# Linear attention and a swish feed-forward layer in one kernel: sums of phi(k) by row tiles, and the k-v products two groups earlier

## The chip, the cores and the metric

The kernel runs on one core of a Trainium2 chip. The metric is the device time of one execution in microseconds (us). Seven runs of the kernel before the change gave a median of 289.71 us (288.77 to 290.61). The profile shown here is of one more execution, which took 289.96 us; the span from its first to its last recorded instruction is 288.2 us. All times of the trace are counted from the start of that span.

## The reference

Eight batches, eight heads, 576 tokens and a head width of 64 go through linear attention, and its result through a feed-forward layer (4608 tokens, width 512, inner width 2048):

```python
q_p, k_p = (phi(q), phi(k))               # phi(x) = elu(x) + 1
kv = np.einsum('bhsd,bhse->bhde', k_p, v)
z = np.sum(k_p, axis=2)
num = np.einsum('bhsd,bhde->bhse', q_p, kv)
den = np.einsum('bhsd,bhd->bhs', q_p, z)[..., None] + 1e-06
x = num / den                             # heads side by side: 4608 x 512
h = x @ w_in
g = h * (1.0 / (1.0 + np.exp(-beta * h)))
out = g @ w_out
```

## The kernel before, in words

**Layout.** A batch's 576 tokens are cut into G = 64 groups of J = 9 tokens. Two heads stand on the 128 partitions (64 groups each), and two pairs of heads ("pr" 0 and 1) make up the four head pairs together with the index h. `phi_k` of a batch is a tile of 128 partitions by (pr, j, 128 columns): rows 0 to 63 belong to one head (hh = 0), rows 64 to 127 to another (hh = 1), and the 128 columns hold two more halves (h = 0, 1) of 64 channels each.

**Products of k.** `k_quads` (L177) walks over j, h and hh and multiplies a 64x64 quadrant of `phi_k`, as the weights, with a moving operand of 64 rows. One call is 36 matmuls, each with a weight load of its own. It serves three purposes: `z_products` (L189, batches 0 and 1 only) uses a single column of ones and so sums phi(k) over the tokens; `kv_direct` (L205, batches 0 and 1) multiplies with v; `kv_both` (L224, batches 2 to 7) multiplies with v that has a column of ones beside it, so that one product gives both kv and z.

**Order.** The order of the instructions is written out by hand (manual_schedule), engine by engine in the order of the code. There are three parts:

- The opening (L547 to L689), batch 0: phi of q and k, transposes of phi(q) (`q_trans`), `z_products` (L578 and L583) and `kv_direct` (L580, L645) with dummy matmuls (`idle`) between them, then the numerators by token tiles (`numer_mm`, L593), their division on DVE (`numer_norm`), the transposes of x (`x_part`, L618) and the first four groups of h = x w_in in pieces (`h0_part`, L628).
- Batch 0's second matrix product (`y_mm`, L447) interleaved with the attention of batch 1 (L708 to L756): `q_trans(1, ...)` at L715 and L718, both `z_products(1, pr)` at L723, `kv_direct(1, pr)`, the denominators (`dens`), the numerators (`numer0`, divided on DVE at L392), the transposes of x (`x_trans1`, copied by ACT at L413), and the four output copies `y_out` (L460, DVE copies L239). `y_sb` has three buffers, so the fourth output copy waits for the first one's DMAs.
- The loop over b = 1 to 8 (L799), in which each H phase (`h_phase`, 16 groups of four 512-column matmuls and a Silu on ACT) and each Y phase (`y_phase`) carries pieces of the attention of batch b + 1 and b + 2. `at(sh, n, ...)` hangs a piece behind group n of H, `at(sy, n, ...)` behind step n of Y. `kv_both(n)` hangs behind group index 10 (the eleventh group), `numers(n)` and the divisions `norms(n, k)` behind the last; `x_trans_dma` sends x through transposing DMAs on SP's queue. For b = 2 the left-over tokens of batches 0 and 1 (`odd_numers`, `odd_norms`) hang ahead of kv_both at index 10, and their four transposing DMAs at index 11.

Instructions are fetched while the kernel runs: the page lists a queue q8 of the kind "instruction" with 20 packets and 0.33 MB. PE's program has 2548 weight loads and 2548 matmuls, by far the longest of the engines.

PSUM has four buffers of one bank that H and Y share (`mmps`), and two small pools for the attention. In the loop the odd numerators (`nps_m`) take two of the four shared buffers until `norms(n, 2)` has read them on DVE; the third token tile of Y waits for that. `norms(n, 2)` needs a fourth and fifth `xs` buffer, and the fifth is free when the first transposing DMA of x (`xT<-xs`) has landed.

**Loads.** POOL issues the loads of q, k, v and the weights that convert to bf16 (queue q0); SP issues the transposing DMAs, the outputs and the loads of v from batch 3 on (queue q1). `load_kq(m + 1)` is held until batch m's transposes of phi(q) (`qTd`, L269) have landed.

Of the kernel before, what the change touches and what calls it, by code (L numbers as in the profile page):

```python
# [16 lines left out]
def kernel(  # L17
# [10 lines left out]
    nc = tc.nc  # L28
# [7 lines left out]
    G = 64  # L36
    J = S // G
# [72 lines left out]
    ones = consts.tile([P, 2], BF16)  # L110
# [27 lines left out]
    st = {}  # L138
# [23 lines left out]
    def places(b, pr):  # L162

        return slice(2 * pr, 2 * pr + 2) if b < 2 else slice(pr, 4, 2)
# [6 lines left out]
    def v_copy(eng, b, pr):  # L171
        src = vb[b % 2] if b == 2 else vf[b % 2]
        eng.tensor_copy(  # L173
            vaug[b % 2][:, pr, :, :, 0:D], src[:, places(b, pr)].rearrange("p h j d -> p j h d")
        )

    def k_quads(b, pr, dst, mov):  # L177

        for j in range(J):
            for h in range(2):  # L180
                for hh in range(2):
                    r = slice(hh * G, (hh + 1) * G)
                    c = slice(h * D, (h + 1) * D)
                    nc.tensor.matmul(  # L184
                        dst[hh][c], st[b, "k"][r, pr, j, c], mov(r, j, h),
                        start=(j == 0), stop=(j == J - 1), skip_group_check=True,
                    )

    def z_products(b, pr, ps):  # L189

        k_quads(b, pr, [a[:, 256 + pr : 257 + pr] for a in ps], lambda r, j, h: ones[r, 0:1])

    def z_evac(b, ps):
        for hh in range(2):
# [26 lines left out]
    def num_tile(name):  # L221
        return numps.tile([P, 2, 512], F32, tag="num", name=name)

    def kv_both(b):  # L224

        t = num_tile("kvp")
        for pr in range(2):
            k_quads(
                b, pr, [t[:, hh, pr * EA : (pr + 1) * EA] for hh in range(2)],
                lambda r, j, h: vaug[b % 2][r, pr, j, h, 0:EA],  # L230
            )
        st[b, "kvd"] = work.tile([P, 2, 2 * EA], BF16, tag="kv_bd", name="kvd")
        nc.vector.tensor_copy(st[b, "kvd"], t[:, :, 0 : 2 * EA])  # L233
# [32 lines left out]
    def q_trans_dma(b):  # L266
        st[b, "qTd"] = work.tile([P, 4 * J, G], BF16, tag="qT", name="qTd")
        for hh in range(2):
            st[b, "qTd", "dma"] = nc.sync.dma_start_transpose(  # L269
                out=st[b, "qTd"][:, hh * 2 * J : (hh + 1) * 2 * J],  # L270
                in_=st[b, "q"][hh * G : (hh + 1) * G].rearrange("p a j c -> p (a j c)"),
            )

    def q_odd_trans(b, tp):

        tv = tp.rearrange("p (a n) -> p a n", a=2)
        for pr in range(2):
            nc.tensor.matmul(
                tv[:, pr], st[b, "q"][:, pr, J - 1, :], identity,
                is_transpose=True, start=True, stop=True, skip_group_check=True,  # L280
            )
        nc.scalar.copy(
            q_odd[b].rearrange("p (i a) g -> p a i g", i=2),
            tv.rearrange("p a (i g) -> p a i g", i=2),
        )
# [30 lines left out]
    def numers(b):  # L316
        pairs = [num_tile("nps") for _ in range(2)]
        odd = [mm_tile("nps_m") for _ in range(2)]
        for k in range(2):
            dst = [pairs[k][:, h] for h in range(2)]  # L320
            numer_tile(b, dst, k)
            numer_tile(b, dst, 2, (k,), 4)
        numer_tile(b, odd, 3)
        for hh in range(2):
            quads(b, odd, 4 + hh, lambda c: (c, J - 1), hh, None)
        st[b, "nps"] = pairs, odd
# [36 lines left out]
    def norms(b, k):  # L363

        den = work.tile([P, 2, 6], F32, tag="den", name="den")
        rden = work.tile([P, 2, 6], F32, tag="rden", name="rden")
        pairs, odd = st[b, "nps"]
        if k < 2:
            nv = pairs[k][:, :, 0 : 6 * EA].rearrange("p h (n e) -> p h n e", e=EA)
            nc.vector.tensor_scalar(den, nv[:, :, :, D], 1e-6, None, ALU.add)  # L370
            nc.vector.reciprocal(rden, den)
            x = xs_tile(b, k).rearrange("p (h n) d -> p h n d", h=2)
            scale(x, nv[:, :, 0:4, 0:D], rden[:, :, 0:4])
            if k == 0:
                xs_tile(b, 2)
            x = st[b, "xs", 2].rearrange("p (h n) d -> p h n d", h=2)
            scale(x[:, :, 2 * k : 2 * k + 2], nv[:, :, 4:6, 0:D], rden[:, :, 4:6])
            return
        nv = [a[:, 0 : 6 * EA].rearrange("p (n e) -> p n e", e=EA) for a in odd]
        for h in range(2):  # L380
            nc.vector.tensor_scalar(den[:, h], nv[h][:, :, D], 1e-6, None, ALU.add)
        nc.vector.reciprocal(rden, den)
        x = xs_tile(b, 3)
        for h in range(2):
            scale(x[:, 4 * h : 4 * h + 4], nv[h][:, 0:4, 0:D], rden[:, h, 0:4])
        x = xs_tile(b, 4)
        for h in range(2):
            scale(x[:, 2 * h : 2 * h + 2], nv[h][:, 4:6, 0:D], rden[:, h, 4:6])
# [9 lines left out]
    def x_dst(b, t):  # L398
        if t < NT - 1:
            return xT[b % 3][:, :, t * P : (t + 1) * P]  # L400
        return xT_tail[:, :, b * G : (b + 1) * G]
# [15 lines left out]
    def x_trans_dma(b, t):  # L417
        xv = st[b, "xs", t].rearrange("p n d -> p (n d)")
        if t < NT - 1:
            nc.sync.dma_start_transpose(out=x_dst(b, t), in_=xv)  # L420
            return

        for pr in range(2):
            nc.sync.dma_start_transpose(
                out=xT_tail[:, places(b, pr), b * G : (b + 1) * G],
                in_=xv[pr * G : (pr + 1) * G, 0 : 2 * P],
            )
# [39 lines left out]
    def load_kq(b, after=None):  # L467
        if b < B:
            d = load(nc.gpsimd, xq[b % NX], q, b)
            if after is not None:  # L470
                hold(d, after)
            load(nc.gpsimd, xk[b % NX], k, b)

    def load_v(b):
        if b < B:
            load(nc.sync, vf[b % 2], v, b)

    def phi_all(b, a):
        phi_tile(b, a)
        for pr in range(2):  # L480
            phi_part(b, a, pr, xin(b, a, pr))
        for pr in range(2):
            phi_relu(b, a, pr, xin(b, a, pr))
        for pr in range(2):
            phi_min(b, a, pr)
# [90 lines left out]
    idle(3)  # L576
    zt = [num0_tile() for _ in range(2)]
    z_products(0, 0, zt)  # L578
    idle(2)
    kv_direct(0, 0, kvp0)  # L580
    for hh in range(2):
        kv_evac(0, hh, (0,), kvp0)
    z_products(0, 1, zt)  # L583
    bps = miscps.tile([P, FC], F32, tag="misc", name="bps")
    nc.tensor.matmul(bps, beta_row, ident16, is_transpose=True, start=True, stop=True)
# [137 lines left out]
    for pr in range(2):  # L723
        z_products(1, pr, zt1)
# [46 lines left out]
    def h_phase(b, x, side):  # L771
        for ff in range(FC):
            hp = mm_tile("h_ps")
            h_mm(b, x, ff, hp)
            silu(b, ff, hp)
            run(side, ff)
# [18 lines left out]
    def at(side, n, *fs):  # L795
        side.setdefault(n, []).extend(fs)


    for b in range(1, B + 1):  # L799
        n = b + 1  # L800
        sh, sy = {}, {}
        if b == 1:
            at(sh, 0, lambda: q_trans_dma(2))
            at(sh, 1, lambda: [v_copy(nc.gpsimd, 2, pr) for pr in range(2)])
            at(sh, 2, lambda: q_odd_trans(1, num_tile("qop")[:, 0].bitcast(BF16)[:, 0:256]))
            at(sh, 2, lambda: load_kq(3, st[2, "qTd", "dma"]), lambda: load_v(3))
        if b == 2:
            at(sh, 10, odd_numers, odd_norms)
            at(sh, 11, lambda: [x_trans_dma(i, 4) for i in range(2)])
        if n < B:  # L810
            at(sh, 10, lambda: kv_both(n))
            at(sh, FC - 1, lambda: numers(n), lambda: [norms(n, k) for k in range(3)])
            for t in range(NT):
                at(sy, t // 3, lambda t=t: x_trans_dma(n, t))
        if n + 1 < B:
            m = n + 1
            at(sy, 3, lambda: phi_all(m, "q"))
            at(sy, 5, lambda: q_trans_dma(m), lambda: load_kq(m + 1, st[m, "qTd", "dma"]))
            at(sy, 8, lambda: phi_all(m, "k"), lambda: [v_copy(nc.gpsimd, m, pr) for pr in range(2)])
            at(sy, 9, lambda: load_v(m + 1))  # L820
        h_phase(b, xT[b % 3] if b < B else xT_tail, sh)
        y_phase(b, sy, last=(b == B))
# [30 lines left out]
```

## Time and profile before

| what | us |
|---|---|
| median of 7 runs | 289.71 |
| the profiled execution | 289.96 |
| its span | 288.2 |
| PE busy | 278.7 (97%) |
| ACT busy | 161.3 (56%) |
| DVE busy | 106.2 (37%) |
| POOL busy | 36.8 (13%) |
| PE on the chain that ended last | 88% |
| matmuls of H (L432), share of that chain | 41% |
| matmuls of Y (L450), share of that chain | 40% |

A busy PE is one on which some matmul is recorded; matmuls are pipelined, so a duration of 0.17 us for one matmul does not mean that the next starts 0.17 us later. The time per matmul in a run of equal ones is read from where the run starts and ends: the run's length, less one matmul's duration, divided by their number less one. "issue" as the reason of an idle stretch means that the engine waited for nothing that the profile records. The granted TensorE clock is 1.0 throughout.

### The profile page before, as it was taken

To read this page: it belongs to the slowest core of one execution; us is meant where nothing else is said; L and a number is where in the kernel's file an instruction comes from. 1 tells how busy PE (TensorE), PEld (TensorE's weight loads), DVE (VectorE), ACT (ScalarE), POOL (GpSimd) and SP (SyncE) were. 2 spreads that over 40 slices of the span, in tenths; PEclk is the share of its full clock that TensorE was granted. 3 is DMA by queue.
4 is the path that set the end of the run, shared out by engine and by line. 5 is a ranking of instruction groups with operands and counts; after the bars stand their busy time and mean duration, and the time that the engine had idled before them with its cause. 6 is when DMAs were issued, how large, how long until landed. Compare 5 with 4: busy or idle time off the path is not lost.

```text
span 288.2 us, 6079 instructions
## 1 busy us (share of the span) xinstructions
PE 278.7 (97%) x2548; PEld 136.3 (47%) x2548; DVE 106.2 (37%) x255; ACT 161.3 (56%) x220; POOL 36.8 (13%) x51
## 2 busy tenths in 40 slices
PE   7879998999999999999999999999999999999994
PEld 3574457444444444444445444544454444444443
DVE  5833577535531491039203930293026100110012
ACT  5758775975736852776287717770860086017500
POOL 8632000220013001300140007000000000000000
PEclk9999999999999999999999999999999999999999
DMA  7999999679389728953796379638403410230032
GB/s 219 208 217 392 247 252 170 148 206 218 73 185 282 128 64 176 295 93 79 166 288 107 82 163 282 116 77 131 104 2 81 114 36 0 48 81 19 0 75 74
DMA packets 51725, 41.05 MB, mean 142 GB/s; under 512 B 31585, under 2 KB 43121, under 8 KB 51697
## 3 DMA queue, kind: packets, MB, share of 16 engines
q1 hardware_dynamic: 38800, 23.61, 34.4%
q0 software_dynamic: 12736, 16.91, 29.8%
q8 instruction: 20, 0.33, 0.5%
q10 hardware_dynamic: 160, 0.13, 0.2%
q14 instruction: 9, 0.07, 0.1%
HBM read 36.71 MB, written 9.44 MB: 160 GB/s over the span
## 4 chain that ended last, share of the span: by engine, by line
PE 88%; DMA 6%; DVE 2%; ACT 1%; issue 1%; SPq 0%; DVEq 0%; POOLq 0%
PE h_ps L432 41%; PE y_ps L450 40%; DMA xk<-in_k_dram 2%; DMA xT<-xs 2%; PE kvp L184 2%; DMA out_dram<-y_sb 1%; PE h_ps L632 1%; PE nps L303 1%; DVE xs L392 1%; DVE y_sb L239 1%; PE nps L184 1%; PE warm_ps L133 0%; ACT g L440 0%; PE nps_m L303 0%; ACT e L144 0%
## 5 line engine op out<-in xcount | busy, mean ns | idle before, releaser
L440 ACT ACTIVATE g<-h_ps,beta_c 128x512 bf16<-128x512 f32 x144 | 97.9, 689 | 92.8 <-PE h_ps L432 92.4
L450 PE MATMUL y_ps<-w_out,g 128*128 128x512 bf16 (+3 forms) x600 | 127.4, 371 | 1.3 <-issue 0.9
L432 PE MATMUL h_ps<-xT,w_in 128*128 128x512 bf16 x496 | 109.8, 379 | 0.6 <-ACT xT L413 0.2
L450 PEld LDWEIGHTS <-g 128*128 128x128 bf16 x600 | 57.6, 98 | 65.7 <-issue 1.0
L432 PEld LDWEIGHTS <-w_in 128*128 128x128 bf16 x560 | 54.2, 98 | 65.1 <-issue 1.3
L239 DVE COPY y_sb<-y_ps 128x512 f32<-128x512 f32 (+2 forms) x37 | 24.8, 674 | 76.0 <-PE y_ps L450 72.9
L83 POOL DMA_DIRECT2D xq<-in_q_dram x7 | 5.2, 744 | 109.5 <-ACT g L440 97.0
L144 ACT ACTIVATE e<-xk 128x1152 bf16<-128x1152 bf16 x16 | 17.8, 1152 | 1.7 <-DMA xk<-in_k_dram 1.5
L233 DVE CAST kvd<-kvp 128x260 bf16<-128x260 f32 x6 | 2.6, 426 | 41.5 <-PE kvp L184 41.5
L144 ACT ACTIVATE e<-xq 128x1152 bf16<-128x1152 bf16 x14 | 15.5, 1155 | 0.1
L432 PE MATMUL h_ps<-xT_tail,w_in 128*128 128x512 bf16 x64 | 14.0, 379 | 0.0
L155 DVE TENSOR_TENSOR phi_q<-e,r 128x1152 bf16<-128x1152 bf16 (+2 forms) x17 | 11.7, 717 | 2.7 <-ACT e L144 2.4
L361 DVE TENSOR_TENSOR xs<-nps,rden 128x512 bf16<-128x512 f32 (+1 forms) x24 | 12.2, 552 | 0.4
L155 DVE TENSOR_TENSOR phi_k<-e,r 128x1152 bf16<-128x1152 bf16 x16 | 11.6, 751 | 0.6 <-ACT e L144 0.4
L173 POOL CAST vaug<-vf 128x1152 bf16<-128x1152 f32 x10 | 11.2, 1160 | 2.0 <-DMA vf<-in_v_dram 2.0
L370 DVE TENSOR_SCALAR den<-nps 128x12 f32<-128x12 f32 x12 | 2.0, 164 | 25.4 <-PE nps L303 25.4
L144 ACT ACT_TABLE_LOAD x6 | 7.7, 1283 | 3.4 <-DMA xq<-in_q_dram 3.4
L133 PE MATMUL warm_ps<-xT 128*128 128x512 bf16 x23 | 8.2, 504 | 1.5 <-DVE xT L96 1.5
L184 PEld LDWEIGHTS <-phi_k 64*64 64x64 bf16 x720 | 6.9, 107 | 4.4 <-issue 3.0
L361 DVE TENSOR_TENSOR xs<-nps_m,rden 128x256 bf16<-128x256 f32 (+1 forms) x24 | 7.0, 349 | 4.2 <-DMA xT<-xs 3.4
L440 ACT ACT_TABLE_LOAD x6 | 7.7, 1283 | 0.1
L83 POOL DMA_DIRECT2D xk<-in_k_dram x9 | 6.8, 751 | 4.5 <-DMA g<-in_moe_w_out_dram 1.9
(93 smaller groups left out, 118.0 us busy)
## 6 DMA issues: line engine op xcount, KB each, us to landing
out_dram<-y_sb SPq DMA_DIRECT2D x70, 128.0 KB, 2.4
vf<-in_v_dram SPq DMA_DIRECT2D x5, 1152.0 KB, 6.6
xq<-in_q_dram POOLq DMA_DIRECT2D x7, 576.0 KB, 9.7
xk<-in_k_dram POOLq DMA_DIRECT2D x7, 576.0 KB, 12.3
w_in<-in_moe_w_in_dram POOLq DMA_DIRECT2D x4, 512.0 KB, 12.8
g<-in_moe_w_out_dram POOLq DMA_DIRECT2D x2, 1024.0 KB, 17.3
stage<-in_moe_w_out_dram POOLq DMA_DIRECT2D x2, 1024.0 KB, 19.7
stage<-in_q_dram SPq DMA_DIRECT2D x2, 576.0 KB, 4.1
```

The lines of the kernel that those rows point to most:

```text
L83: return eng.dma_start(out=dst[:, h0 : h0 + n].rearrange("p h j d -> p h (j d)"), in_=rows.rearrange("(i p) e -> p i e", p=P)[:, h0 : h0 + n],
L133: nc.tensor.matmul(warm_ps[:, 0:cols], warm[:, 0:P], warm[:, 0:cols], start=True, stop=True)
L144: nc.scalar.activation(st[b, a, pr, "e"][:, :, j0:j1], x[:, :, j0:j1], ACTF.Exp)
L155: nc.vector.tensor_tensor(st[b, a][:, pr, j0:j1].rearrange("p j (h d) -> p j h d", h=2), st[b, a, pr, "e"][:, :, j0:j1].rearrange("p h j d ...
L173: eng.tensor_copy(vaug[b % 2][:, pr, :, :, 0:D], src[:, places(b, pr)].rearrange("p h j d -> p j h d"))
L184: nc.tensor.matmul(dst[hh][c], st[b, "k"][r, pr, j, c], mov(r, j, h), start=(j == 0), stop=(j == J - 1), skip_group_check=True,)
L239: eng.tensor_copy(dst, src)
L303: nc.tensor.matmul(dst[h][c * G : (c + 1) * G, e * EA : (e + 1) * EA], st[b, "qTd"][r, (hh * 2 + p) * J + j, :], st[b, "kvd"][r, hh, p * E ...
L361: nc.vector.tensor_mul(out, num, rd[..., None].to_broadcast(list(num.shape)))
L432: nc.tensor.matmul(hp[:, c0:c1], w_in_sb[ff // 4][:, kc, (ff % 4) * P : (ff % 4 + 1) * P], x[:, kc, c0:c1], start=(kc == 0), stop=(kc == K ...
L440: nc.scalar.activation(g_sb[b % 2][:, ff, :], hp, ACTF.Silu, scale=beta_c[:, ff : ff + 1])
L450: nc.tensor.matmul(yp[:, c0:c1], g_sb[b % 2][:, ff, t * P : (t + 1) * P], w_out_sb[i][:, c, c0:c1], start=(ff == 0), stop=(ff == FC - 1), ...
```

## The change

`z_products` no longer goes through `k_quads`. It takes 64 rows and all 128 columns of `phi_k` as weights (a row tile), so that both halves h are summed by one matmul: 18 weight loads and 18 matmuls per call where there were 36 of each. There are four calls (batches 0 and 1, two pr each), so PE's program loses 72 weight loads and 72 matmuls. Sums, PSUM places and the instructions that read them (`z_evac`) are the same.

In the loop, `kv_both(n)` moves from behind group index 10 of H to behind index 8, that is from the eleventh to the ninth group, for all b from 1 to 6. For b = 2 `odd_numers` and `odd_norms` move along with it, and the four transposing DMAs of the left-over tokens move from index 11 to 9. `numers(n)` and everything in Y stay.

```diff
     def z_products(b, pr, ps):
 
-        k_quads(b, pr, [a[:, 256 + pr : 257 + pr] for a in ps], lambda r, j, h: ones[r, 0:1])
+        for j in range(J):
+            for hh in range(2):
+                r = slice(hh * G, (hh + 1) * G)
+                nc.tensor.matmul(
+                    ps[hh][:, 256 + pr : 257 + pr], st[b, "k"][r, pr, j, :], ones[r, 0:1],
+                    start=(j == 0), stop=(j == J - 1), skip_group_check=True,
+                )
...
         if b == 2:
-            at(sh, 10, odd_numers, odd_norms)
-            at(sh, 11, lambda: [x_trans_dma(i, 4) for i in range(2)])
+            at(sh, 8, odd_numers, odd_norms)
+            at(sh, 9, lambda: [x_trans_dma(i, 4) for i in range(2)])
         if n < B:
-            at(sh, 10, lambda: kv_both(n))
+            at(sh, 8, lambda: kv_both(n))
```

## The prediction

> **What bounds the kernel now.** I read the page first (PE busy 97%, 88% of the chain), then the chain of waits in order of time. From 75.33 us to the end the chain is PE without a break, one H and Y phase after another, and the change takes no PE work out of that stretch. So what it is worth is decided before 75.33 us. There the chain has these pieces (start, length, what):
>
> ```profile
> 15.33 0.17 PE nps L598 x3
> 15.50 1.37 issue
> 16.86 0.23 PE nps L598
> ...
> 48.69 0.61 DVE y_sb L239
> ...
> 49.91 3.90 DMA out_dram<-y_sb
> ...
> 53.92 0.69 DVE y_sb L239
> ...
> 55.04 0.70 ACT g L440
> ...
> 68.70 6.26 DMA xT<-xs
> 74.96 0.02 issue
> 74.98 0.30 DVE xs L361
> 75.28 0.05 issue
> 75.33 0.82 PE y_ps L450 x3
> ```
>
> Two DMA waits and one idle stretch of PE with no cause on record stand out. The timeline of PE has that stretch and a second one; the other two rows price small matmuls:
>
> ```profile
> 9.86 0.45 PE L184 MATMUL nps<-ones,phi_k 64*64 64x1 bf16 x36 [0.71 <-DVE phi_k L155]
> 12.30 0.54 PE L513 MATMUL dps<-z,qT 128*128 128x2 bf16 x16
> 16.86 0.23 PE L598 MATMUL nps<-kv,qT 128*128 128x128 bf16 x1 [1.37 <-issue]
> 49.51 0.60 PE L450 MATMUL y_ps<-w_out,g 128*128 128x256 bf16 x4 [0.89 <-issue]
> ```
>
> Counted in PE's program (each weight load and each matmul a row), 446 rows precede the first stall and 1,213 the second: 767 apart. The page explains the number:
>
> ```profile
> q8 instruction: 20, 0.33, 0.5%
> ```
>
> 20 packets carry the 5,096 rows, about 256 each; 767 is three times 256 less one wait instruction of PE's sequencer in between. So I read both stalls as PE at the edge of a block of instructions that has not arrived. PE began the blocks before these (rows 190 and 957) at 10.98 and 43.73 and could go on at 16.86 and 49.51: a block arrives 5.8 to 5.9 us after PE has begun the one before it, while loads fill the DMA engines. PE normally takes far longer for 256 rows (108 ns per row in Y, 27 us), but the small matmuls use up rows quickly.
>
> The second stall has a sequel. The DMA view of 50 to 53 us:
>
> ```profile
> q1 hardware_dynamic: 154, 0.25, 36.8%
> q8 instruction: 1, 0.02, 3.6%
> ...
> out_dram<-y_sb SPq DMA_DIRECT2D x3, 128.0 KB, 3.9
> ```
>
> 3.6% of 16 engines over 3 us is 1.7 us: one engine is held by one instruction packet, and the output DMAs of that moment need 3.9 us where the page's median is 2.4. The fourth output copy waits for them (53.92), so does phi of batch 2 on DVE behind it, then `qTd`, then the held loads of batch 3, then the first `xT` (74.96), then Y's third tile (75.33), which PE would have reached 0.45 us earlier.
>
> **The change, part by part.** Block edges stay at the same row numbers; 36 rows of work after each `z_products` come earlier.
>
> *Edge at row 446.* Row 190, which asks for it, is now in the second `z_products`, at 11.3 (it waits for phi_k as before), so the block is there at 17.2. Row 446 is now in `x_part(1, 1)`, which ran at 18.83, without the stall 17.46. The stall of 1.37 us goes. What is late next: w_in lands in time (20.02 for the third quarter, wanted at 23.4), but `q_trans(1)` needs phi_q of batch 1, whose last DVE piece ends at 38.00 because the load of xq landed at 33.63. PE came to it at 38.72. So of 1.37 only 0.66 us reaches batch 1; 0.71 us is slack, which also covers a dearer `z_products` in batch 0.
>
> *Row tiles.* 36 quadrant matmuls take (0.45 - 0.167)/35 = 8 ns each, since four quadrants work side by side: 0.29 us a call. No row of the trace has a 64x128 weight tile. Below: two side by side at half the quadrants' rate is 16 ns, half of the full-array row (dps: (0.54 - 0.163)/15 = 25 ns) 12.5 ns. Above: a whole weight load unhidden, 98 ns (the LDWEIGHTS 128x128 rows). I take 25 ns, the nearest row, whose weights also have 128 columns: 0.45 us a call, +0.16 us. Batch 0's two calls (+0.32) vanish in the slack; batch 1's two cost +0.32. There `kv_direct` follows at once, now with another tile shape: by the chain 72 quadrant matmuls cost 0.71 to 0.73 us where they follow full tiles (kvp) and 0.67 where they follow quadrants (kv), so +0.06. The quadrants' 8 ns per pair shows that weight loads are mostly hidden here. The Trainium skill ("TensorE: Matmul & The Clock Gate", "LDWEIGHTS (loading the stationary operand)") speaks against the change: a load's time goes with its columns, whatever its rows, so half as many loads of twice the columns save nothing; its 107 ns, two side by side, would make a call 0.96 us (an estimate), and the gain of the whole change about 0.1 us.
>
> *Edge at row 957.* Before, row 702 came in plain Y work long ahead. Now it follows `q_trans(1)` at about 38.5, so the block arrives by 44.4 at the latest; PE reaches row 957, near the end of `kv_direct(1)`, at about 44.1. A stall of 0 to 0.3 us; I take 0.15.
>
> *Edge at row 1213.* It moves from the opening into `kv_both(2)`, at some 59 us; the block is there long before. The stall before 49.51 goes: `x_trans1(3)` ran at 50.60 and would have run at 49.56, so 1.04 us. The Trainium skill ("Runtime: NRT & Kernel Launch", "Instruction fetch mechanics") has the blocks of 256 but calls crossing an edge mostly hidden; by that the fewer rows would be worth nothing. The two stalls above say otherwise here.
>
> Sum at `x_trans1(3)`: -0.66 + 0.32 + 0.06 + 0.15 - 1.04 = **-1.17 us**. ACT behind it (copy, exp of k, table load, first Silu, which ended at 55.73 and set H's fifth group at 55.77) shifts alike. PE then reaches Y's third tile at 74.88 - 1.17 = 73.71.
>
> *The DMA side must keep up.* With no block asked for at 49.5, the output DMAs issued at 49.91 - 0.13 should land after 2.4 us, at 52.18 in place of 53.80: the fourth copy starts at 52.3 (-1.62), phi of batch 2, `qTd`, the loads of batch 3 and the landing of `xT` follow by the same: 74.96 - 1.62 = 73.34, and 0.35 us of DVE later the third tile is free at 73.69. So PE's 73.71 sets it, just: 75.33 - 73.71 = **1.62 us gained**.
>
> *kv two groups earlier.* No PE work changes; 16 rows and 1.73 us come between kvp and numers, so that 256 rows across both take at least 7 us, over the 5.9 a block needs. What kvp waits for: vaug of batch 3 ends on POOL at 88.85, kvp would start at 91.99 - 1.73 = 90.26; the later batches have 2 us to spare. In b = 1, phi_k(2) ends at 59.54 - 1.62 = 57.9 and kvp comes at about 59.0; even at the old phi it would wait under 0.6 us, which the third tile's idle time covers. A waiting kvp would hold up H's next group on PE, and Silu on ACT behind it. The four transposing DMAs of b = 2 keep SP busy for 5.58 us from 91.4 in place of 93.10; behind them stand batch 3's at 98.78, which gain 1.7 us of room. DVE has 9 us idle there. I cost this part at nothing; without that room a wait on vaug would cost at most the 1.73 us, once.
>
> **In time.** The profiled execution took 289.96, so 288.3; it lies 0.25 above the median, 289.71. Against that: **288.1 us**.
>
> **Rivals.**
> - *More.* The packet at 32.95 on q8 moves to about 39 us, so xq of batch 1 may land up to 0.95 us sooner, and row tiles may run at 12.5 ns. Then up to 0.6 us less wait and 0.45 us cheaper tiles: as far as the DMA side follows, 287.0 to 287.6. 0.10.
> - *Absorbed.* The output DMAs at 50 us stay at 3.9 us for another reason (loads of v still running until 50.31), and the chain through `xT` moves by 0.1 to 0.3 us only: 289.5. For it: the last load packets and the outputs are close. Against: 2.4 us everywhere else. 0.20.
> - *Slower: weight loads of row tiles not hidden.* With p us each (p over 0.036, where the slack is used up), `x_trans1(3)` shifts by 72p - 3.50 us: four calls of 18, less 144 quadrants at 8 ns (1.15), less 1.37 and 1.04, plus 0.06. The third tile's idle time covers 0.45 of it. It loses from 55 ns each, by over 0.3% from 67 ns, and at 98 ns by 3.1 us: 292.9. Against it: 25 ns with full tiles. 0.08.
>
> The forecast case itself (287.7 to 288.7) has 0.62. 0.3% is 0.87 us, about what a measurement of this kernel can tell from no change: faster by more than that 0.71 (forecast, more), within it 0.20, slower 0.09. The range takes in the first two rivals and tiles of up to 55 ns, and leaves out the slow end: 286.9 to 289.7.
>
> **What would show it.** Right: no idle "issue" near PE rows 446 and 1213; q8 packets no longer between 50 and 53 us; output DMAs there at 2.4 us; the fourth y_sb copy near 52.3; Y's third tile of b = 1 near 73.7 (the 1.62 us); from there on the same spacing of phases (29.3 us) as before. Wrong: 18 row tiles over 0.6 us; a stall of the old size at the new edges; `xT` still landing near 75; kvp waiting for POOL or DVE in any batch.

## The result, and the profile after

| | before | after |
|---|---|---|
| median, us | 289.58 (47 runs, 288.77 to 291.42) | 287.36 (20 runs, 287.06 to 287.91) |
| ratio of the times | 1 | 0.9918, 95% interval 0.9905 to 0.993 |
| the profiled execution, us | 289.96 | 287.37 |
| its span, us | 288.2 | 285.6 |
| weight loads, and as many matmuls | 2548 | 2476 |

The change is worth 2.22 us by the medians and 2.59 us between the two profiled executions (the one of before lay 0.38 above its median). The granted clock has a part in the medians. Of the 82 runs of the kernel before that stand beside the experiments, 29 had a mean granted clock of 0.994 or less and a median of 290.68 us, the other 53 one of 289.30; of the 20 runs of the changed kernel one was at 0.994. At the full clock the change is thus worth some 1.9 us (an estimate, 289.30 less 287.36). One run of the experiments below, at a clock of 0.754 (363.84 us, with quadrants in batch 1), is left out there. The forecast was 288.1 us, 0.74 too high, with 286.9 to 289.7 around it.

The page of the changed kernel has one packet fewer on the instruction queue:

```profile
q8 instruction: 19, 0.31, 0.4%
```

PE's timeline of the opening, where before had 1.37 us of idle "issue" (start, busy time, instruction, and in brackets the idle time ahead of it with its releaser):

```profile
9.57 0.38 PE L194 MATMUL nps<-ones,phi_k 64*128 64x1 bf16 x18 [0.33 <-DVE phi_k L155]
...
10.96 0.38 PE L194 MATMUL nps<-ones,phi_k 64*128 64x1 bf16 x18
...
14.42 0.62 PE L638 MATMUL h_ps<-xT,w_in 128*128 128x128 bf16 x8 [0.25 <-DMA w_in<-in_moe_w_in_dram]
14.87 0.39 PE L604 MATMUL nps<-kv,qT 128*128 128x128 bf16 x4
```

The four matmuls of `numer_mm` (L604) run through with no idle time ahead of them; row 446 now comes at 17.00, in `x_part(1, 1)`. The two `z_products` show the row tile: 18 in 0.38 us, so (0.38 - 0.160)/17 = 12.9 ns each (one such matmul lasts 0.160 us), and the run of 36 below gives (0.60 - 0.160)/35 = 12.6.

The same view around the second stall:

```profile
42.56 0.60 PE L194 MATMUL nps<-ones,phi_k 64*128 64x1 bf16 x36
43.09 0.78 PE L184 MATMUL kv<-vf,phi_k 64*64 64x64 bf16 x72
...
48.41 0.60 PE L456 MATMUL y_ps<-w_out,g 128*128 128x256 bf16 x4
48.85 0.39 PE L414 MATMUL tp<-identity,xs 128*128 128x128 bf16 x4
```

Nothing idle: `x_trans1(3)` starts at 48.85, where it was at 50.60. The DMA view of 50 to 53 us has no row for q8 any more, and the output DMAs are back at the median of the page:

```profile
q1 hardware_dynamic: 364, 0.61, 88.2%
...
out_dram<-y_sb SPq DMA_DIRECT2D x5, 128.0 KB, 2.4
```

DVE's timeline has the fourth output copy 2.2 us sooner (before: 53.92), and it waits 1.90 us for the first one's DMA:

```profile
51.69 0.69 DVE L245 COPY y_sb<-y_ps 128x512 f32<-128x512 f32 x1 [1.90 <-DMA out_dram<-y_sb]
```

The chain of waits, in order of time (start, length, what):

```profile
33.86 1.28 ACT L144
...
35.15 2.23 ACT e L144 x2
...
37.40 0.77 DVE phi_q L155
...
38.22 0.51 PE nps L265 x6
...
49.76 2.22 ACT e L144 x2
...
53.29 0.70 ACT g L446
...
54.03 4.48 PE h_ps L438 x20
58.50 0.73 PE kvp L184 x72
...
66.12 13.92 PE y_ps L456 x64
```

At 38.22 PE now waits for `phi_q` of batch 1: the slack of the prediction, used up. H's fifth group of b = 1 starts at 54.03 (before: 55.77). Y of b = 1 runs from 66.12 through its third tile without a wait (xT landed at 71.95; before, 74.96); kvp of batch 2 waits for nothing. The profile's 2.6 us therefore come from three places: 1.75 by `x_trans1(3)`, 0.61 at the third tile (in before it began 0.61 us later than the matmuls' own spacing gives), and 0.2 in b = 2, where before had small holes of PE among the numerators at row 2235 and the changed kernel has none.

### The profile page after: what moved, and what is told of

Same layout as the page of the kernel before. It is cut to its first block, busy times and chain, and to the rows that moved or that the text cites. A ratio compares the mean times of both kernels' runs of the same rounds, so it can differ in the third digit from the quotient of the medians.

```text
span 285.6 us, 5935 instructions
## 1 busy us (share of the span) xinstructions
PE 277.4 (97%) x2476; PEld 135.6 (47%) x2476; DVE 106.1 (37%) x255; ACT 161.1 (56%) x220; POOL 37.0 (13%) x51
## 4 chain that ended last, share of the span: by engine, by line
PE 84%; DMA 10%; ACT 3%; POOL 1%; issue 1%; DVE 0%; POOLq 0%; ACTq 0%
PE y_ps L456 41%; PE h_ps L438 38%; DMA xq<-in_q_dram 8%; DMA vf<-in_v_dram 3%; ACT e L144 2%; PE kvp L184 1%; PE nps L309 1%; PE nps_m L309 0%; ACT L144 0%; POOL xk L83 0%; PE nps L265 0%; PE nps L536 0%; ACT L446 0%; DVE phi_q L155 0%; PE kv L184 0%
## 5 line engine op out<-in xcount | busy, mean ns | idle before, releaser
L367 DVE TENSOR_TENSOR xs<-nps,rden 128x512 bf16<-128x512 f32 (+1 forms) x24 | 12.2, 552 | 0.8 <-DMA xT_tail<-xs 0.4
L133 PE MATMUL warm_ps<-xT 128*128 128x512 bf16 x23 | 7.6, 474 | 1.5 <-DVE xT L96 1.5
L367 DVE TENSOR_TENSOR xs<-nps_m,rden 128x256 bf16<-128x256 f32 (+1 forms) x24 | 7.1, 350 | 3.7 <-DMA xT<-xs 3.3
L703 DVE TENSOR_SCALAR w_out<-g,rbeta 128x512 bf16<-128x512 f32 x8 | 3.8, 536 | 8.8 <-DMA g<-in_moe_w_out_dram 8.8
```

The lines of the kernel that those rows point to most:

```text
L133: nc.tensor.matmul(warm_ps[:, 0:cols], warm[:, 0:P], warm[:, 0:cols], start=True, stop=True)
L367: nc.vector.tensor_mul(out, num, rd[..., None].to_broadcast(list(num.shape)))
L703: nc.vector.tensor_scalar(w_out_sb[i][:, c, :], w_out_f[i][:, c, :], rbeta[:, ff : ff + 1], None, ALU.mult,)
```

## The experiments

Each was timed beside the kernel before, in three groups, in which its median was 289.44, 289.34 and 289.69 us (at a granted clock of 0.997 or more 289.20, 289.30 and 289.30). The changed kernel (287.36) was timed apart from them. **My theory**: PE ran dry at block edges at which small matmuls had used up 256 rows faster than the next block came, the second fetch also slowed DMAs, and moving the edges is the gain. **Rivals**: the number of PE instructions counts; the tiles' own speed counts; or kv's new place brings the gain.

### The two halves of the change

**Row tiles alone** (kv back at index 10, left-over tokens at 10 and 11):

```diff
-            at(sh, 8, lambda: kv_both(n))
+            at(sh, 10, lambda: kv_both(n))
```

> Row tiles alone, kv_both left in the eleventh group. Edge theory (the gain comes from where the edges of PE's 256-row instruction blocks fall in the opening, which only the row tiles move): as the changed kernel, 287.2 to 287.8, no idle PE near 15.5 and 48.4 us. Rival kv (the earlier place of kv earns a good part of the gain): 288.2 or more.

Measured: 288.22 us (287.27 to 288.56, 6 runs), ratio 0.9944 (0.9921 to 0.9966). Above what I expected of my theory (287.2 to 287.8), and where I expected the rival kv (288.2 or more); of six runs two lay near 287.4 and four between 288.1 and 288.6. The profiled execution (287.45) has no stall at either edge and no wait at the third tile, though xT landed at 72.66, 0.7 us later than in the changed kernel.

**The place of kv alone** (the kernel before with kv at index 8, the left-over tokens at 8 and 9):

```diff
-            at(sh, 10, lambda: kv_both(n))
+            at(sh, 8, lambda: kv_both(n))
```

> kv_both in the ninth group alone, sums of phi(k) by quadrants. Edge theory: both stalls (1.4 us near 15.5, 1.0 us near 48.4) and the wait of the fourth output copy stay; only the 0.2 us at the edge at row 2235, among numers of batch 3, goes: 289.2 to 289.6. Rival kv: 288.5 or less.

Measured: 289.27 us (288.84 to 290.6), ratio 0.9982 (0.996 to 1.0004). As expected: both stalls stay (0.80 us idle "issue" in `numer_mm`, 1.16 ahead of `x_trans1(2)`). That the first is shorter than the 1.37 us of before goes with the clock: in this execution the granted clock was 0.5 from 12.50 to 15.91 us, so PE came to the edge at 16.35 (before: 15.50).

So the tiles carry the gain, and the two halves give more together (2.22) than singly (1.2, or 1.5 when timed again below, and 0.2). I had costed kv's place at nothing. My new theory: with the tiles in, the DMA side has no room left, and kv's place moves an instruction fetch out of its way. Three kernels ask for that.

**Row tiles alone, again** (the same code as the first):

> The row tiles alone once more: its first six times fell in two groups (287.3 to 287.5 and 288.1 to 288.6). Theory 'chance of the third tile': with kv in the eleventh group the instruction fetch of that place runs at about 59.8 to 60.9 us, beside the transposes of phi(q) of batch 2 and the loads of batch 3, so that xT lands at 72.7 or later and Y's third tile of b = 1 waits in some executions by up to 0.9 us: again times on both sides, median 287.8 to 288.3. Rival 'the place is worth nothing, as forecast': median 287.2 to 287.6, the earlier times having been chance.

Measured: 287.82 us (287.32 to 290.46, 12 runs), ratio 0.9945 (0.9921 to 0.9969). Both groups again, six runs on each side of 288.0. This time the profiled execution (287.63) shows the wait, in the chain and on PE:

```profile
66.73 6.12 DMA xT<-xs
...
72.88 0.30 DVE xs L367
...
73.22 6.87 PE y_ps L456 x31
```

```profile
73.22 4.06 PE L456 MATMUL y_ps<-w_out,g 128*128 128x512 bf16 x18 [0.31 <-DVE xs L367]
```

Read backwards: the third tile waits 0.31 us for DVE's `norms(n, 2)` (L367), that for xT, which landed at 72.85. By the matmuls' own spacing (0.216 us) the tile is 0.47 us late. The DMA view of 59 to 62 us of this kernel has the fetch, and that of the changed kernel does not (there it came at 58.25 to 59.2):

```profile
q1 hardware_dynamic: 832, 0.75, 88.4%
q8 instruction: 1, 0.02, 2.1%
```

The fetch ran from 59.77 to 60.80; the second `qTd`, which took 3.75 us in the kernel before (58.57 to 62.32, no fetch beside it), took 4.56 in the changed kernel and 5.37 here. It landed at 61.99 (changed kernel: 61.23), so the held load of q of batch 3 went out at 62.52 (61.77), that of k landed at 72.37 (71.42), and xT behind it at 72.85 (71.95). The other traces agree: of the fourteen in all, eight have no fetch between 55 and 63 us, and their second `qTd` took 3.75 to 3.88 us; six have one, and theirs took 4.54 to 5.37. In every trace xT landed 0.5 to 0.8 us behind k of batch 3.

**Only kv of batch 2 late**, and its counterpart **only kv of batch 2 early**:

```diff
-            at(sh, 8, lambda: kv_both(n))
+            at(sh, 10 if b == 1 else 8, lambda: kv_both(n))
```

> The changed kernel with only kv of batch 2 (in b = 1) back in the eleventh group; batches 3 to 7 and the left-over tokens stay in the ninth. If what kv's place is worth is decided at 58 to 73 us (fetch beside the transposes of phi(q) and the loads of batch 3), this behaves like the row tiles alone: 287.8 to 288.3, with the fetch near 59.8 and xT landing at 72.6 or later. If it is decided in later batches or is nothing: 287.2 to 287.6.

```diff
-            at(sh, 8, odd_numers, odd_norms)
-            at(sh, 9, lambda: [x_trans_dma(i, 4) for i in range(2)])
+            at(sh, 10, odd_numers, odd_norms)
+            at(sh, 11, lambda: [x_trans_dma(i, 4) for i in range(2)])
...
-            at(sh, 8, lambda: kv_both(n))
+            at(sh, 8 if b == 1 else 10, lambda: kv_both(n))
```

> The changed kernel with kv of batch 2 in the ninth group, and kv of batches 3 to 7 and the left-over tokens back in the eleventh and twelfth. If b = 1 decides: like the whole change, 287.2 to 287.6, with the fetch near 58.3 and xT landing at 72.0. If a later batch decides: 287.8 to 288.3. If the place is worth nothing: 287.2 to 287.6 and the other two kernels likewise.

Measured: late 288.17 us (287.35 to 290.19, ratio 0.9954, 0.9934 to 0.9974), early 287.45 us (286.98 to 290.64, ratio 0.9948, 0.9923 to 0.9974). The intervals of the ratios do not separate them; the counts do. Over 288.0 us were 17 of 30 runs of the three kernels with batch 2's kv late (4 of 6, 6 of 12, 7 of 12), and 3 of 32 with it early (0 of 20, 3 of 12). It is not the clock that parts them: among the runs at a granted clock of 0.997 or more it is 15 of 28 against 1 of 29. The traces agree: late, the fetch came at 59.76, xT landed at 72.89 and the tile waited 0.33 (0.49 late by the spacing); early, 58.27, 72.05 and no wait. It is the one call of `kv_both` in b = 1 that counts; the other five and the left-over tokens are worth nothing that can be seen. In the profiled executions the tile is late by 0 to 0.49 us. That this grows to the 0.7 to 1 us by which the upper group lies higher is argued, since no execution of that group was profiled.

### The edges

One reading of all fourteen traces bears on this. PE has eight idle stretches of "issue" between matmuls that are longer than 0.1 us: two each in the kernel before, kv alone and the freed output copy, one each in the two kernels below that put edges back, none in the other nine. All eight stand at row 446 or 1213, and each ends 1.3 to 1.6 us after a packet on q8 has ended (before: packets to 15.26 and 48.13, PE goes on at 16.86 and 49.51). Where PE came to one of the edges from row 446 to row 1213 and did not idle, the packet had ended at least 1.67 us earlier. This is what blocks that arrive late would look like.

**More rows, no row tiles**: the kernel before with 92 more loads and matmuls, of 8 columns, in the idle opening.

```diff
-    idle(15)
+    idle(102, 8)
+    idle(5)
```

> The kernel before with 92 more weight loads and matmuls in the opening's dummy stretch (102 of 8 columns and 5 of 512 in place of 15 of 512): 184 rows more, so that the edges fall on about the same work of batch 0 as in the changed kernel (256 - 184 = 72). Sums by quadrants, kv in the eleventh group. Edge theory: faster than before though PE has more to do, 287.5 to 288.3. Rival count: 289.6 or slower.

Measured: 288.23 us (287.9 to 290.57, 12 runs), ratio 0.9965 (0.9947 to 0.9982). With 184 rows more PE is faster than before by some 1.2 us (1.0 at a granted clock of 0.997 or more), as the edges say, and the rival of the number of instructions falls. Its timeline at the place of the second stall, quadrants and all:

```profile
48.51 0.39 PE L408 MATMUL nps<-identity,xs 128*128 128x128 bf16 x4
48.73 0.60 PE L450 MATMUL y_ps<-w_out,g 128*128 128x256 bf16 x4
49.17 0.39 PE L408 MATMUL tp<-identity,xs 128*128 128x128 bf16 x4
```

**Both edges put back** into the changed kernel: 72 rows in the opening and 72 in batch 0's Y (matmuls of 512 columns cut in two).

```diff
-    idle(15)
+    idle(6)
+    idle(45, 102)
...
-            y_mm(0, t, i, yps[t])
+            y_mm(0, t, i, yps[t], n=2)
...
-    y_mm(0, 0, 2, yps[0])
-    y_mm(0, 1, 2, yps[1])
+    y_mm(0, 0, 2, yps[0], n=2)
+    y_mm(0, 1, 2, yps[1], n=2)
```

> The changed kernel with its block edges put back on the work where they were before: 36 more weight loads and matmuls in the opening's dummy stretch (51 of fewer columns in place of 15 of 512, the same columns in all) and 36 matmuls of Y of batch 0 cut into halves of 256 columns (72 rows more, 36 x 2.5 ns). Row tiles and kv's early place are kept. Edge theory: both stalls return, the fourth copy waits for an output DMA of some 3.9 us again, 289.1 to 289.5. Rival count (fewer and cheaper PE instructions earn the gain, wherever the edges lie): 287.4 to 287.7.

Measured: 288.35 us (288.15 to 288.64, 7 runs), ratio 0.9955 (0.9938 to 0.9972): only 1.0 of the 2.2 us came back, so this missed. Of the first edge it says little. In the profiled execution the first stall stayed away, but PE was late there for two reasons. The rows that I put into the opening stood ahead of `z_products`, and PE then waited 0.99 us for phi_k (0.33 in the changed kernel); and the granted clock was 0.5 from 12.24 to 15.65 us, as the page's row of 40 slices shows:

```profile
PEclk9899999999999999999999999999999999999998
```

So PE came to row 446 at 16.69, 1.78 us after the packet (13.94 to 14.91) had ended. At the full clock it would have come about 1 us sooner (an estimate: w_in landed at 15.00, and the first piece of h began at 16.12), which is before the block was ready by the 1.3 to 1.6 us above. The other six runs, all at a clock of 1.0, were not profiled. What reached batch 1 of the two delays was 0.56 us. The second stall came back at half its size, and behind it output DMAs of 2.85 to 3.1 us:

```profile
49.01 0.61 PE L458 MATMUL y_ps<-w_out,g 128*128 128x256 bf16 x4 [0.53 <-issue]
```

**The second edge alone**: 144 rows in batch 0's Y (matmuls cut in two and four), the opening as in the changed kernel.

```diff
-            y_mm(0, t, i, yps[t])
+            y_mm(0, t, i, yps[t], n=4 if i else 2)
...
-    y_mm(0, 0, 2, yps[0])
+    y_mm(0, 0, 2, yps[0], n=4)
```

> The changed kernel with 144 more PE rows in batch 0's Y (some 512-column matmuls cut into two or four of the same total), so that the block edge at row 1213 falls again where small work has used the rows up quickly; the first edge stays as in the changed kernel. Edge theory: a stall of 0.5 to 1.1 us near 48.4, output DMAs of 2.8 to 3.9 us behind it, and cut matmuls that cost 0 to 0.2 us: 287.9 to 288.8. Rival 'number of instructions': 144 rows at 0.02 us each or less, no stall at that place, 287.4 to 287.8.

Measured: 287.92 us (12 runs, ratio 0.9945, 0.9925 to 0.9965), 0.56 above the changed kernel: just in the range of the edges (287.9 to 288.8), above that of the number of instructions (287.4 to 287.8). The stall is there, and slow output DMAs with a q8 packet beside them in the view of 49 to 54 us:

```profile
50.35 0.60 PE L458 MATMUL y_ps<-w_out,g 128*128 128x256 bf16 x4 [0.58 <-issue]
```

```profile
q8 instruction: 1, 0.02, 1.5%
...
out_dram<-y_sb SPq DMA_DIRECT2D x5, 128.0 KB, 3.1
```

The profiled execution was the longest of the twelve (289.96; the others 287.63 to 288.47). In it w_in landed at 15.95, PE waited 1.94 us for that, and the granted clock was 0.5 from 15.39 to 18.80 us. The late w_in alone does not make it so long: the next kernel's profile has it too, at the full clock, and took 287.90. So I read from this one the stall, not the length.

**Quadrants again in batch 0 only, and in batch 1 only**:

```diff
     def z_products(b, pr, ps):
 
+        if b == 0:
+            k_quads(b, pr, [a[:, 256 + pr : 257 + pr] for a in ps], lambda r, j, h: ones[r, 0:1])
+            return
```

> The changed kernel with quadrants in batch 0's two z_products again (72 PE rows more, all ahead of row 446), row tiles in batch 1 alone. Edge theory: row 446 falls into numer_mm again, so PE stalls by 1.0 to 1.5 us near 15.5; what arrives is that less the slack of 0.77 us that PE spends waiting for phi_q of batch 1 in the changed kernel, so that wait is gone and q_trans(1) comes 0.4 to 0.7 us later; the second edge then lies where batch 1's 72 rows fewer leave it, in plain work, without a stall. 287.8 to 288.3. Rival 'batch 0 is slack altogether': 287.2 to 287.5.

Measured: 288.00 us (287.42 to 289.19, 12 runs), ratio 0.9939 (0.9915 to 0.9962): 0.64 above the changed kernel, as the first edge, worth 0.60 behind its slack, says. That is by the times alone. The profile does not show the stall itself: w_in landed late in this execution too (16.13) and PE had already waited 1.87 us for it when it came to row 446.

The other kernel has `if b == 1:` in the same place.

> The changed kernel with quadrants in batch 1's two z_products again, row tiles in batch 0 alone. Edge theory: no stall near 15.5; 72 rows fewer ahead of row 1213 put that edge into the work behind x_trans1(3), where a matmul takes 216 ns, so no stall near 48.5 either; the price is batch 1's z_products, 0.67 us in place of 0.53. 287.4 to 287.9. If the row tiles' own speed in batch 1 were what counts, with no stall gone there: 288.3 or more.

Measured: 287.32 us (five runs, 287.25 to 287.69), ratio 0.9915 (0.9882 to 0.9948), no different from the changed kernel. No stall near either edge. Batch 1's `z_products` with quadrants take 0.67 us in the chain, with row tiles 0.53 or 0.54. The tiles' own speed is thus worth 0.1 us in the chain. Batch 0's 72 rows fewer are enough to take both stalls away; batch 1's alone, in the kernel above, bring most of the gain too and leave 0.64 us, that of the first edge.

### The sequel, and what is late next

**The fourth output copy freed**: the kernel before, which copies it into the idle `stage` tile.

```diff
-        y_out(0, t, yps[t])
+        y_out(0, t, yps[t], y_sb=stage[:, 0:DM] if t == 3 else None)
```

> The kernel before, with batch 0's fourth output copied into the free stage tile in place of the first y_sb buffer, so that it does not wait for the output DMAs that the instruction packet slows. Both stalls of PE stay. Theory of the sequel: the copy starts at 52.3 to 52.9 in place of 53.92, phi of batch 2, qTd, the loads and xT come some 1 us sooner, Y's third tile of b = 1 does not wait, H's fifth group stays at 55.8: 0.45 to 0.65 us faster, 288.8 to 289.2. Rival 'the wait is set elsewhere': unchanged, 289.4 to 289.7.

Measured: 289.18 us (288.8 to 291.57), 0.5 below the median of before beside it, but the ratio is 0.9997 (0.9971 to 1.0023): by the times alone not settled. The profile (289.07) shows the sequel. The copy starts at 51.23 (expected: 52.3 to 52.9), three output DMAs still take 3.2 to 3.5 us, H's fifth group stays late at 55.54, and the third tile of Y no longer waits.

**q of batch 1 one place earlier on POOL's queue**, in the changed kernel:

```diff
-    for i in range(3):
+    for i in range(2):
         load_w_out(i)
     load(nc.gpsimd, xq[1], q, 1)
+    load_w_out(2)
...
-    for i in range(3):
+    for i in range(2):
         w_out_scale(i, 0)
...
     phi_all(1, "q")
+    w_out_scale(2, 0)
     phi_all(1, "k")
```

> The changed kernel with the load of q of batch 1 one place earlier on POOL's queue, ahead of the third quarter of w_out, whose scaling moves behind phi of q. q_trans(1) then need not wait for phi_q: 0.77 us sooner on PE. But ACT takes e of batch 2's q when its load lands (44.8) and is then busy nearly without a gap until the first Silu; the gaps sum to 0.2 to 0.3 us. If ACT is what is late next: 287.0 to 287.3. If PE's 0.77 us came through: 286.5 to 286.8.

Measured: 286.86 us (286.48 to 287.84, 6 runs), ratio 0.9901 (0.9869 to 0.9933): 0.50 below the changed kernel, between my two expectations. The load lands at 31.15 (33.79), PE does not wait, and H's fifth group starts at 53.20 (54.03). So most of PE's 0.77 us came through, and what is late next shows in the chain:

```profile
23.28 21.38 DMA xq<-in_q_dram
...
44.74 2.22 ACT e L144 x2
...
46.98 1.16 ACT xT L419 x3
```

From the landing of q of batch 2 at 44.66 on (23.28 and 21.38), ACT works almost without a gap until the first Silu. I had summed its gaps as 0.2 to 0.3 us and left out that a group of copies written as 1.25 us holds waits for PE (2.50 us for four became 2.16 without them).

## Why the prediction was right, and where its sizes were off

**The time.** 287.36 us lies inside the range of 286.9 to 289.7, but not in the forecast case's own 287.7 to 288.7: the stalls went as forecast, and the gain was larger, for the reasons below.

**What bounds.** Right: the gain falls ahead of Y's third tile of b = 1, except for 0.2 us in b = 2.

**Edge at row 446.** Right. The stall went, `q_trans(1)` ran into phi_q (idle 0.77), and the chain at `y_mm` behind it came 0.60 sooner (38.73 for 39.33; forecast 0.66).

**Row tiles: the term that was mis-sized.** I took 25 ns a pair, the full-array row, from the bounds 12.5 to 98; the chip showed the low end, 12.6 to 12.9. Batch 1's two calls and `kv_direct` behind them cost -0.14 + 0.04 in place of +0.32 + 0.06: 0.48 us of the error. The Trainium skill ("TensorE: Matmul & The Clock Gate", "LDWEIGHTS (loading the stationary operand)") has a load go with its columns; my estimate from its figure was 0.96 us a call, and the 0.38 us measured for one decides against using it here.

**Edge at row 957.** I took 0.15 us and it cost nothing: its block was fetched at 40.71 to 41.67 and PE reached the row at 43.65.

**Edge at row 1213.** Right: 1.04 us gone. The sum at `x_trans1(3)` became -0.60 - 0.14 + 0.04 - 1.04 = -1.74 (measured -1.75; forecast -1.17). The Trainium skill ("Runtime: NRT & Kernel Launch", "Instruction fetch mechanics") calls the crossing of blocks mostly hidden; here two of them cost PE 1.4 and 1.0 us, and 184 more rows in the right place took both away.

**The DMA side.** Right, it kept up: output DMAs 2.3 us (forecast 2.4), the fourth copy at 51.69 (52.3), xT at 71.95 (73.34), third tile at 72.97 (73.71; 32 matmuls behind 66.05), for which the way was free at 72.32 (0.37 us behind xT, as in before), 0.65 us ahead. I had read the idle time there as the 0.45 us that the view put down to DVE; from the spacing of starts it was 0.61, and all of it went.

**kv two groups earlier: the step that failed.** "I cost this part at nothing" held for each wait that I named, and by itself it is worth nothing sure. But the forecast had the third tile set by PE "just", with 0.02 us to spare, and I did not ask what kv's move does to that margin. It moves a fetch by 1.5 us, and without it about half of the executions are longer: some 0.7 us on the median (288.08 over the 18 runs of tiles alone, against 287.36). Of the three profiled executions with batch 2's kv late, one has 0.01 us of the margin left, and in two the tile is late by 0.47 and 0.49 us.

**The rivals.** *More* (287.0 to 287.6) is where the time fell, by its second reason, tiles near 12.5 ns; its first did not happen, since the fetch did move from 32.95 to 40.71 but q of batch 1 landed at 33.79, not sooner than 33.63. *Absorbed* fell with the output DMAs at 2.3 us, *Slower* with the tiles (its time at 98 ns is 292.8 by its own sum, not 292.9).

What stays open: why a fetch delays the transposes by 0.8 us at one time and 1.6 at another, and the size of the third tile's wait in the longer executions. Open too is why the kernel before so often runs at the lower granted clock (29 of 82 runs, against 1 of 20), which makes up some 0.3 of the 2.22 us; no run asks for that. The profile names no cause for PE's idle "issue". That it is a missing block rests on the q8 times, the same 1.3 to 1.6 us in all eight stalls, and on stalls that go and come as rows are added in several places.

## What to carry to other kernels

Idle time of PE that the profile puts down to "issue" is worth setting beside the times of the instruction queue: where small matmuls spend some 256 rows within a few microseconds, a different number of rows ahead of that place can take the stall away, and more rows can do as well as fewer. Where a forecast ends with two sides within a few hundredths of a microsecond of each other, each remaining edit is to be asked what it does to that margin, however idle it looks. Before a gap of a microsecond is explained, the granted clock of the execution that shows it is to be read: here it most likely hid one stall, and it went with the longest execution of another kernel. And a small matmul without a row of its own was priced best here by its share of the array: half of it took half of the full array's 25 ns (a quarter took 8, so no rule comes of it).

## What the runs showed of the hardware

- Small matmuls with a weight load each, pair by pair: 8 ns for 64x64 quadrants, 12.6 to 12.9 for 64x128 row tiles, 25 for the full array with two columns. A row tile sums twice the channels of a quadrant, so it is the cheaper by channel.
- One instruction packet of about 16 KB (0.31 MB in 19) took 0.9 to 2.0 us in the fourteen traces, and transfers that ran beside it ended later: output DMAs of 2.3 us took 2.8 to 4.2, the second transpose of phi(q) 4.54 to 5.37 us in place of 3.75 to 3.88. It is not the only cause: with q of batch 1 moved, the first three output DMAs took 3.24 to 2.67 us with no packet beside them, while a load of v ran until 50.31.
- The first quarter of w_in landed at 14.2 to 15.2 us in twelve of the fourteen profiled executions, and at 15.95 and 16.13 in two, with PE waiting 1.9 us for it.
- In four of the fourteen profiled executions (kv alone, both edges back, the second edge alone, 184 rows more) the granted clock was 0.5 for 3.4 us at a stretch, somewhere between 12.2 and 18.8 us; their mean clock was 0.991 to 0.994.
